# Attention values and scores of two pairs per visit in a fused attention and feed-forward kernel

## The chip, the core and the metric

The kernel runs on one core of a Trainium2 chip. The metric is the device time of one execution in microseconds (us). Engines are named as the profile names them: PE (TensorE, matmuls; PEld is its loading of weights), DVE (VectorE), ACT (ScalarE), POOL (GpSimd) and SP (SyncE, which issues most of the DMAs).

## What is computed

```python
def _attn_ref(q, k, v):                      # 8 x 8 heads x 576 x 64, float32
    scores = scale * np.matmul(q_c, k_c.transpose(0, 1, 2, 4, 3))   # in chunks of 64
    scores = scores - np.max(scores, axis=-1, keepdims=True)
    attn = np.exp(scores)
    attn = attn / (np.sum(attn, axis=-1, keepdims=True) + 1e-09)
    return np.matmul(attn, v_c)
def _moe_ref(x, w_in, w_out):                # 4608 x 512, 512 x 2048, 2048 x 512
    h = x @ w_in
    g = h - np.tanh(h)
    return g @ w_out
```

The attention is local: each chunk of 64 positions attends to itself alone. Its result, with the heads side by side, is the input x of the feed-forward part.

## The kernel before

The 4608 tokens are 36 **pairs** (two chunks of 64 tokens, 128 rows, with all 8 heads) and 9 **groups** of four pairs (512 tokens). Attention of a group runs one group ahead of its feed-forward part. Each float32 operand is split into a high and a low float16 part, and each matrix product is made of three of the four part products.

Up to the middle of group 2 all engines follow two orders written out by hand, as tokens (`PLAN` and `SECOND`). In `SECOND` the token `S16` is the scores of pair 16, `a17` the load of q and k of pair 17, `K13` a chunk, `gq3` the last product X5 of a unit, and so on. From group 3 (`LATER`) to group 8 the loops at L953 to L978 run, and there only PE's order is the order of the program text (`manual_schedule(engines={E.PE})`, L952). The other engines' orders are put together by the framework before the kernel runs, from what is ready and from the order of the text; each engine then works through its own queue strictly in that order.

A group has four **units** (`unit`, L750). The first feed-forward product uses seven products per quarter of the hidden columns instead of eight (Strassen and Winograd). They are named here by bank and first operand: Y1, X0, Z3, Z6, X4, Y2, X5 (`product`, L681, 12 matmuls of 256 columns each). X, Y and Z are three PSUM banks. X4 and X5 add to the sum in X, Z6 adds to Z; X0, Y1, Z3 and Y2 start anew. Four **shrinks** per unit (`shrink`, L690) take the sums out: `copied` (L705, ACT, from Y or Z), `summed` (L709, DVE, from X), `tanh` (L713, ACT), `less` (L717, DVE), `high` (L723, ACT) and `low` (L727, DVE). So X4 has to wait until shrink 0 has read X, X5 until shrink 1 has, and Z6 until `middle` (L679, ACT) has copied Z. A **chunk** (L731, 12 matmuls of 512 columns, two output tiles) is the second feed-forward product of one shrink's result, taken from a list that holds the results of three shrinks.

Between the third chunk and X5 stands the **attention visit** of pair p (L963 to L972):

- the values of p (`crossed_products`, L418): 48 matmuls of 64 x 64 (L427), into columns 256 to 511 of a pair of banks, of which one is Z and the other is used by attention alone;
- the scores of pair p + 1 (`scores`, L359; L183): 32 float32 matmuls in the trace, into columns 0 to 255 of the same two banks;
- the results of p (`results`, L442): a copy out of PSUM (L450, ACT), and sums and differences for x of the next group, split into parts (L454, L460 to L465, ACT and DVE);
- the softmax of p + 1: maxima (L374) and differences (L378) on DVE, exponentials (L387) on ACT, sums, reciprocals and products (L393 to L396) on DVE, high and low part (L405 on ACT, L410 on DVE), a transposing DMA (L415, SP);
- the loads of q and k of pair p + 3 (L304, SP).

At the start of the unit the values of p are split (L349 on ACT, L353 on DVE), and those of p + 4 are loaded (L308, SP); at its end their largest value is taken (L315, DVE), and once per group a power of two is made of these (`powers`, with an all-reduce on POOL, L116). Two buffers hold the split values, two the transposed shares, two the loaded q and k.

Of the kernel before, what the change touches and what calls it, by code (L numbers as in the profile page):

```python
# [52 lines left out]
"""  # L53

SECOND = """
v8 0i12 v9 W0.2 wA v11 0j12 x 0k12 0P14 xA 0G11 v10 0i11 0q12 wB 0P12 0j11 xB C0.0 W1.4 W1.8 W1.7 0k11 Cx1 C1.0 Cx0 0q11 f D0.0 Dx1 0P11 C1.6 Dx0 C0.1 G0 C0.3 D0.1 G1 D1.0 C1.3 e1 C1.5 C1.1 i0 D0.3 j0 C0.2 e0 D1.1 k0 C0.9 a8 C0.6 e2 G3 o1 u11 e3 q0 o0 W0.13 W0.10 P0 u10 u9 a9 i3 D0.6 i1 W1.10 j3 j1 k1 C0.5 u8 D1.6 q1 G6 C1.8 C1.7 W0.7 W0.8 k3 i6 D0.5 D1.3 C1.10 P1 M D0.9 C0.10 S8 o2 D1.5 W1.2 a10 G9 C1.9 j6 k6 C0.7 rA2 q3 P3 D1.10 i9 m8 D1.7 q6 E8 G5 C1.4 C0.13 j9 D0.2 P6 D0.7 k9 G7 C0.8 D1.9 W0.4 W1.13 W1.15 z8 rB2 T0.0.0 T0.0.1 D1.8 i5 q9 j5 W0.14 h8 C1.2 k5 T0.1.1 D0.10 D0.8 C0.4 l8 T0.1.0 C1.13 s8 t8 i7 W1.14 W0.15 s9 D1.2 S9 D1.13 T0.2.1 j7 m9 C0.14 q5 d8 fb P9 D0.13 G10 P5 k7 E9 z9 T0.3.1 T0.2.0 V8 G8 T0.3.0 i10 h9 j10 q7 D1.4 D0.4 P7 W0.12 s10 k10 q10 X8.0 i8 C1.14 C0.15 l9 c0.1 c0.2 d10 j8 D0.15 W1.12 W0.11 C0.12 C1.12 S10 G2 P10 t9 k8 i2 m10 b0.2 E10 q8 c0.0 D0.14 d9 G4 j2 k2 b0.1 V9 z10 P8 D1.12 X8.1 i4 a12 j4 q2 c0.3 h10 a11 X9.0 D1.14 G13 b0.0 s11 X9.1 C1.15 l10 S11 i13 X9.4 b0.3 v14 m11 T1.0.0 P2 X8.2 D0.12 o3 v13 T1.0.1 T1.2.1 X9.2 t10 X9.5 k4 q4 E11 W1.11 G15 i15 z11 X9.6 C1.11 d11 P4 j13 C0.11 v15 h11 l11 X9.7 k13 j15 V10 G14 i14 q13 k15 v12 P13 D1.15 t11 G12 X10.0 V11 u15 u12 T1.1.0 D0.11 j14 D1.11 k14 q15 X9.3 u13 X9.8 i12 X10.1 X11.0 T1.2.0 X10.2 T1.3.0 T1.1.1 q14 T1.3.1 P15 j12 k12 c1.3 u14 rA3 G11 S12 X11.1 q12 m12 X11.5 X11.2 P14 i11 a13 P12 E12 X11.3 rB3 c1.2 z12 j11 X11.4 gz0 s12 h12 k11 c1.0 X11.6 l12 gy0 q11 P11 t12 c1.1 sc0 mc0 ee2 b1.3 b1.0 b1.2 d12 b1.1 gx0 gu0 ee0 X11.7 ee3 V12 st0 sn0 X11.8 oo2 oo3 T2.0.1 su0 ee1 oo1 gv0 X12.0 sc1 a14 st1 gw0 sh0 T2.1.1 S13 sl0 gq0 sc2 T2.3.1 K0 m13 sn1 s14 st2 su1 sn2 sh1 gz1 su2 E13 sl1 z13 X12.1 h13 T2.2.1 st3 gy1 l13 sh2 T2.0.0 t13 sc4 d14 oo0 mc1 K1 s13 gx1 T2.2.0 sl2 sn3 T2.1.0 gu1 st4 T2.3.0 d13 sc5 K2 su3 X12.2 v18 sn4 c2.2 su4 V13 gv1 sh3 X13.0 sl3 sh4 c2.3 st5 gw1 sn5 sl4 K3 S14 c2.0 b2.2 c2.1 b2.3 v17 su5 X13.1 b2.0 gq1 m14 K4 sc6 v16 X13.2 E14 sh5 st6 b2.1 z14 st7 h14 sl5 l14 gz2 mc2 sn6 t14 gy2 a15 K5 u18 T3.0.0 su6 sn7 T3.1.0 T3.0.1 sh6 sc8 X13.4 T3.3.0 T3.1.1 sl6 T3.3.1 u16 gx2 T3.2.1 su7 st8 gu2 s15 u17 T3.2.0 sh7 K6 V14 gv2 sn8 su8 gw2 sc9 c3.0 sl7 sh8 d15 c3.2 sc10 X14.0 K7 st9 b3.0 c3.1 v19 sl8 S15 gq2 sn9 c3.3 K8 X14.1 b3.1 su9 m15 st10 b3.2 gz3 sh9 sl9 st11 sn10 E15 z15 h15 sn11 su10 l15 b3.3 u19 su11 a16 gy3 K9 sc12 mc3 sh10 t15 X13.3 X13.7 rA4 sl10 gx3 gu3 sh11 st12 X13.8 sc13 X13.5 sn12 K10 rB4 sl11 su12 X13.6 V15 gv3 X14.2 X15.0 X15.1 sh12 st13 X15.4 gw3 X15.5 X15.2 sn13 X15.7 X15.3 K11 S16 su13 gq3 sh13 sl12 X15.8 sl13 sc14 m16 st14 X15.6 st15 E16 K12 z16 sn14 sn15 su14 h16 sh14 su15 sh15 K13 a18 l16 sl14 sl15 t16 a17
"""

ORDER = (0, 1, 3, 6, 9, 5, 7, 10, 8, 2, 4, 13, 15, 14, 12, 11)
# [5 lines left out]
def attn_ffn_kernel(ctx: ExitStack, tc: tile.TileContext, qkE, vE, qL, kL, vL, w_in, w_out, out):  # L65
# [597 lines left out]
    class Winograd:  # L663
# [67 lines left out]
        def chunk(self, behind=3):  # L731
# [15 lines left out]
            if last:  # L747
                ff.finish(tiles)
# [277 lines left out]
```

## Time and profile before

| | |
|---|---|
| median of 3 runs | 793.89 us (793.58 to 794.11) |
| profiled execution, its own time | 793.73 us |
| its span, from the first to the last instruction | 792.0 us |
| PE busy | 784.5 us, 99% of the span |
| DVE busy | 610.8 us, 77% |
| ACT busy | 485.3 us, 61% |
| POOL busy | 47.9 us, 6% |

Busy time is the time in which at least one instruction of the engine ran. PE's matmuls overlap, and their ends are modelled, so PE's pace is read from the distance between starts and not from durations. A row of the timeline gives start and duration in us, engine, line, operation, output and inputs by the program's names, shapes and the number of instructions merged into it.

### The profile page before, as it was taken

How to read it: one execution, taken by the hardware profiler on the slowest of the kernel's cores; microseconds unless marked ns; L12 is line 12 of the kernel's file. 1: busy time of each engine (PE TensorE's matmuls, PEld its weight loads, DVE VectorE, ACT ScalarE, POOL GpSimd, SP SyncE). 2: the span in 40 equal slices, each digit the busy share in tenths (PEclk: the TensorE clock that was granted, in tenths of full speed). 3: DMA queues.
4: the chain of work that ended last, by engine and by line, in shares of the span. 5: the costliest groups of instructions: out<-in, count | busy, mean ns of one | idle time of the engine just before them, and what ended most of it. 6: DMA issues, size and time to landing. Idle time of an engine off the chain costs nothing.

```text
span 792.0 us, 17323 instructions
## 1 busy us (share of the span) xinstructions
PE 784.5 (99%) x7178; PEld 519.5 (66%) x7178; DVE 610.8 (77%) x1114; ACT 485.3 (61%) x938; POOL 47.9 (6%) x82
## 2 busy tenths in 40 slices
PE   8999999999999999999999999999999999999998
PEld 4877884444676666666666666666666666666664
DVE  8999999999999997676867686768676777654443
ACT  6989968986675655555645465556455645453443
POOL 0032135500000000000000000000000000000000
PEclk9999999999999999999999999999999999999999
DMA  9887848853131224111311131112211220001001
GB/s 355 321 234 220 222 130 179 150 134 81 28 111 50 81 61 108 47 55 54 108 55 54 55 105 37 50 40 92 68 55 41 68 67 15 15 12 43 1 1 54
DMA packets 58735, 72.43 MB, mean 91 GB/s; under 512 B 32800, under 2 KB 33056, under 8 KB 58528
## 3 DMA queue, kind: packets, MB, share of 16 engines
q1 hardware_dynamic: 53760, 61.81, 24.8%
q0 software_dynamic: 4752, 9.44, 7.0%
q8 instruction: 56, 0.92, 0.5%
q14 instruction: 23, 0.19, 0.1%
q10 hardware_dynamic: 144, 0.07, 0.0%
HBM read 45.09 MB, written 9.44 MB: 69 GB/s over the span
## 4 chain that ended last, share of the span: by engine, by line
PE 88%; DVE 7%; ACT 2%; DMA 2%; issue 1%; SPq 0%; DVEq 0%; ACTq 0%
PE po L746 36%; PE ph L687 23%; PE psa L687 9%; PE po L620 7%; PE ph L575 7%; PE psa L183 2%; PE psa L427 1%; DVE w L153 1%; DVE w L157 1%; DMA raw<-w_out 1%; PE psa L440 1%; DVE wl L164 1%; ACT junk L168 1%; DMA raw<-w_in 1%; DVE w L149 1%
## 5 line engine op out<-in xcount | busy, mean ns | idle before, releaser
L746 PE MATMUL po<-wl,gh 128*128 128x512 f16 x672 | 154.2, 379 | 0.0
L746 PE MATMUL po<-wl,gl 128*128 128x512 f16 (+1 forms) x672 | 151.6, 375 | 0.0
L687 PEld LDWEIGHTS <-wh 128*128 128x128 f16 x1344 | 129.2, 98 | 22.3
L687 PE MATMUL ph<-xh,wl 128*128 128x256 f16 x672 | 114.6, 273 | 0.0
L746 PEld LDWEIGHTS <-gl 128*128 128x128 f16 x720 | 69.1, 98 | 67.3
L687 PEld LDWEIGHTS <-wl 128*128 128x128 f16 x1008 | 98.5, 98 | 21.6
L746 PEld LDWEIGHTS <-gh 128*128 128x128 f16 x672 | 65.7, 98 | 67.3
L687 PE MATMUL ph<-xl,wl 128*128 128x256 f16 x336 | 91.6, 273 | 0.0
L687 PE MATMUL ph<-xh,wh 128*128 128x256 f16 x448 | 76.7, 273 | 0.0
L687 PE MATMUL psa<-xh,wh 128*128 128x256 f16 x448 | 76.4, 273 | 0.0
L620 PE MATMUL po<-wl,gh 128*128 128x512 f16 (+1 forms) x192 | 63.2, 383 | 0.0
L687 PE MATMUL ph<-xl,wh 128*128 128x256 f16 x224 | 61.1, 273 | 0.0
L687 PE MATMUL psa<-xl,wh 128*128 128x256 f16 x224 | 61.0, 273 | 0.0
L713 ACT ACTIVATE t<-t,sig 128x512 f32<-128x512 f32 x37 | 26.6, 719 | 32.9 <-DVE t L709 32.8
L713 ACT ACTIVATE t<-wh,sig 128x512 f32<-128x512 f32 x38 | 27.3, 720 | 31.0 <-DVE wh L709 30.9
L713 ACT ACTIVATE t<-spare,sig 128x512 f32<-128x512 f32 x37 | 26.6, 720 | 30.0 <-DVE spare L709 30.0
L575 PE MATMUL ph<-xl,wl 128*128 128x512 f16 x192 | 43.8, 379 | 0.2 <-DVE t L591 0.2
L454 ACT CAST xh<-wh 128x512 f16<-128x512 f32 (+1 forms) x56 | 31.4, 564 | 11.1 <-DVE wh L461 9.9
L709 DVE TENSOR_TENSOR wh<-ph,wh 128x512 f32<-128x512 f32 x28 | 19.3, 688 | 24.3 <-PE ph L687 24.1
L709 DVE TENSOR_TENSOR t<-ph,t 128x512 f32<-128x512 f32 x28 | 19.2, 687 | 23.4 <-PE ph L687 23.3
L387 ACT ACTIVATE s<-s 128x512 f32<-128x512 f32 x24 | 15.1, 629 | 36.0 <-DVE s L378 36.0
L717 DVE SCALAR_TENSOR_TENSOR wh<-wh,sig,t 128x512 f32<-128x512 f32 x38 | 28.4, 748 | 11.1 <-ACT t L713 11.0
(181 smaller groups left out, 1444.3 us busy)
## 6 DMA issues: line engine op xcount, KB each, us to landing
raw<-w_in SPq DMA_DIRECT2D x16, 512.0 KB, 6.0
raw<-w_out SPq DMA_DIRECT2D x16, 512.0 KB, 6.7
wh<-wl POOLq DMA_DIRECT2D x32, 256.0 KB, 4.2
rawv<-vL SPq DMA_DIRECT2D x28, 256.0 KB, 3.1
rawq<-qL SPq DMA_DIRECT2D x28, 256.0 KB, 3.1
rawk<-kL SPq DMA_DIRECT2D x28, 256.0 KB, 3.5
out<-wh SPq DMA_DIRECT2D x28, 256.0 KB, 2.1
qk<-qkE SPq DMA_DIRECT2D x8, 512.0 KB, 8.7
```

Source lines behind the costliest of these rows:

```text
L149: nc.vector.tensor_single_scalar(w, w, 3, op=ALU.logical_shift_left)
L153: nc.vector.scalar_tensor_tensor(out=w, in0=low, scalar=29, in1=w, op0=ALU.logical_shift_right, op1=ALU.bitwise_or)
L183: nc.tensor.matmul(ps[os, r ^ o if crossed else r, hp * CH:(hp + 1) * CH], lhsT=lhsT(rs, hp, o), rhs=rhs(rs, hp, o), start=True, stop=True)
L387: nc.scalar.activation(s, s, AF.Exp, scale=scale)
L454: return (lambda: nc.scalar.copy(out=h, in_=a)), (lambda: nc.vector.tensor_sub(l, a, h))
L575: nc.tensor.matmul(ph, lhsT=self.weight(fc, 0, a)[:, kc * P:(kc + 1) * P], rhs=x[b][:, kc, cols], start=(k == 0), stop=(k == 3 * KC - 1))
L620: nc.tensor.matmul(self.po[t], lhsT=gg[a][:, ts], rhs=self.weight(fc, 1, b), start=(k == 0), stop=(k == 3 * FC - 1))
L687: nc.tensor.matmul(bank[:, q * 2 * P:(q + 1) * 2 * P], lhsT=self.weight(u, a, i, q, kc), rhs=self.x[j][:, b, kc, :], start=(first and q == ...
L709: nc.vector.tensor_tensor(out=c, in0=self.banks["X"], in1=self.m5 if n % 4 == 3 else c, op=ALU.subtract if n % 4 == 2 else ALU.add)
L713: nc.scalar.activation(t, self.now[n][0], AF.Tanh, scale=self.ff.sig)
L717: nc.vector.scalar_tensor_tensor(out=c, in0=c, scalar=self.ff.sig, in1=t, op0=ALU.mult, op1=ALU.subtract)
L746: nc.tensor.matmul(bank, lhsT=g[a][:, ts], rhs=half_w[1][fc][:, b, columns], start=(first and s == 0 and k == 0), stop=(last and s == 1 an ...
```

## The change

The visit takes two pairs, p and p + 1, in every second unit, and stands at the end of the unit, behind the last chunk: first the values of both, then the scores of the next two. The values of a pair go into one half of the columns of X and one half of Y (pair p in the first, p + 1 in the second), and the copy out of PSUM becomes two of 256 columns. The scores of an odd pair go into columns 256 to 511 of the two banks of the scores. Maxima and differences stand ahead of all steps of the results but the copies out. Splits, loads and largest values come for two pairs at a time; `powers` comes in the third unit of a group instead of the fourth. In the unit the chunks move: one at the start, one cut into two halves (one output tile each) around Z3, one behind Z6, and one at the end; X4 comes ahead of Z6. In `SECOND`, pair 17 gets its load and scores (`a17`, `S17`), and its softmax follows the hand-written part.

```diff
-... u19 su11 a16 gy3 ... K11 S16 su13 gq3 ... sl14 sl15 t16 a17
+... u19 su11 a16 a17 gy3 ... K11 S16 S17 su13 gq3 ... sl14 sl15 t16
...
-        def scores(self, p):
+        def scores(self, p, second=False):
...
-            d["ps"] = quarters(self.two_banks(), lambda r, hp, c: q[r, hp, c, :], lambda r, hp, c: k[r, hp, c, :], "u", self.crossed(p))
+            ps = self.two_banks()
+            d["ps"] = quarters(ps[:, :, 4 * CH:] if second else ps, lambda r, hp, c: q[r, hp, c, :], lambda r, hp, c: k[r, hp, c, :], "u", self.crossed(p))
...
-        def crossed_products(self, p):
+        def crossed_products(self, p, banks):
...
-                        nc.tensor.matmul(ps[os, c, hp * CH:(hp + 1) * CH], lhsT=v[a][rs, c, hp, :], rhs=d["a16"][rs, b, hp, cs], start=(k == 0), stop=(k == 2), skip_group_check=True)
+                        nc.tensor.matmul(banks[c][os, hp, :], lhsT=v[a][rs, c, hp, :], rhs=d["a16"][rs, b, hp, cs], start=(k == 0), stop=(k == 2), skip_group_check=True)
...
+                halves = to.rearrange("p s k (c t) -> p (s k) c t", c=2)
+                return [lambda c=c: nc.scalar.mul(halves[:, :, c], bank[c], 2.0 ** -14) for c in range(2)]
...
-        def chunk(self, behind=3):
+        def chunk(self, behind=3, parts=(0, 1)):
...
             extra("start")
+            self.chunk()
             self.product("Y", u, 1, 1, True)
-            self.chunk()
             self.product("X", u, 0, 0, True)
             self.shrink(u, 0)
+            self.chunk(parts=(0,))
             self.product("Z", u, 3, 3, True)
             self.middle()
+            self.chunk(parts=(1,))
+            self.product("X", u, 4, 4)
+            self.product("Z", u, 6, 2)
+            self.shrink(u, 1)
             self.chunk()
-            self.product("Z", u, 6, 2)
-            self.product("X", u, 4, 4)
-            self.shrink(u, 1)
             self.product("Y", u, 2, 6, True)
-            self.chunk()
-            extra("attention")
             self.product("X", u, 5, 5)
             self.shrink(u, 2)
             self.shrink(u, 3)
             self.chunk()
+            extra("attention")
             extra("end")
...
+    att.softmax(CROSSED + 1)
+    att.transpose(CROSSED + 1)
+    att.load(CROSSED + 3)
...
+                    if u % 2 or p >= NPAIR:
+                        return
+                    two = p, p + 1
+                    later = [n for n in (p + 2, p + 3) if n < NPAIR]
+                    if where == "start":
+                        for n in two:
+                            att.split(n)
+                            att.load_values(n + 4)
+                    elif where == "attention":
+                        for n in two:
+                            att.crossed_products(n, [w.banks[b].rearrange("p (n hp k) -> n p hp k", n=2, hp=4)[n % 2] for b in "XY"])
+                        for n in later:
+                            att.scores(n, n % 2 == 1)
+                        rest = []
+                        for n in two:
+                            steps_ = att.results(n, nx)
+                            for f in steps_[:2]:
+                                f()
+                            rest += steps_[2:]
+                        for n in later:
+                            att.less(n)
+                        for n in later:
+                            att.load(n + 2)
+                        for f in rest:
+                            f()
+                        for n in later:
+                            att.exponents(n)
+                            att.shares(n)
+                            att.transpose(n)
+                    elif where == "end":
+                        for n in two:
+                            att.largest(n + 4)
+                        if u == 2 and later:
+                            att.powers(g + 2)
```

## Rows read from the trace of the kernel before

**Rows 1.** The page, parts 1 and 2: busy time, granted clock of PE.

```profile
PE 784.5 (99%) x7178; PEld 519.5 (66%) x7178; DVE 610.8 (77%) x1114; ACT 485.3 (61%) x938; POOL 47.9 (6%) x82
...
PEclk9999999999999999999999999999999999999999
```

**Rows 2.** The chain that ended last, from 440 to 470 us, by line.

```profile
by line: PE po L746 51.8%; PE ph L687 30.9%; PE psa L687 14.2%; PE psa L183 1.9%; PE psa L427 1.7%
```

**Rows 3.** Timeline of PE from a unit's third chunk on: start, duration, engine, line.

```profile
446.58 2.75 PE L746 MATMUL po<-wl,gl 128*128 128x512 f16 x12
449.27 0.58 PE L427 MATMUL psa<-wh,wh 64*64 64x64 f16 x48
449.72 0.69 PE L183 MATMUL psa<-rawk,rawq 64*64 64x64 f32 x32
450.35 0.39 PE L687 MATMUL ph<-xh,wh 128*128 128x256 f16 x2
...
451.67 2.75 PE L746 MATMUL po<-wl,gh 128*128 128x512 f16 x12
454.26 0.38 PE L687 MATMUL ph<-xh,wl 128*128 128x256 f16 x2
...
455.57 2.75 PE L746 MATMUL po<-wl,gl 128*128 128x512 f16 x12
```

**Rows 4.** Line 450 after 297 us, one per pair: shortest, median, longest ns.

```profile
L450 ACT ACTIVATE wh<-psa x20: 577/578/600, 305.4 to 698.5; 128x512 f32<-128x512 f32 x20
```

**Rows 5.** Timeline of PE, stretches ending at 449.36, 449.65, 449.86 and 450.15 us.

```profile
449.27 0.28 PE L427 MATMUL psa<-wh,wh 64*64 64x64 f16 x11
...
449.27 0.57 PE L427 MATMUL psa<-wh,wh 64*64 64x64 f16 x47
...
449.72 0.35 PE L183 MATMUL psa<-rawk,rawq 64*64 64x64 f32 x9
...
449.72 0.65 PE L183 MATMUL psa<-rawk,rawq 64*64 64x64 f32 x29
```

**Rows 6.** Timeline of DVE behind the same visit.

```profile
451.30 0.42 DVE L460 TENSOR_TENSOR wh<-wh,wh 128x256 f32<-128x256 f32 x1
451.64 0.42 DVE L464 TENSOR_TENSOR wh<-wh 128x256 f32<-128x256 f32 x1
...
456.58 0.67 DVE L393 TENSOR_REDUCE sm<-s 128x8 f32<-128x512 f32 x1
457.17 0.74 DVE L717 SCALAR_TENSOR_TENSOR spare<-spare,sig,t 128x512 f32<-128x512 f32 x1
457.83 0.16 DVE L394 TENSOR_SCALAR sm<-sm 128x8 f32<-128x8 f32 x1
457.95 0.75 DVE L717 SCALAR_TENSOR_TENSOR t<-t,sig 128x512 f32<-128x512 f32 x1
458.62 0.20 DVE L395 RECIPROCAL sm<-sm 128x8 f32<-128x8 f32 x1
```

**Rows 7.** Timeline of ACT behind the same visit.

```profile
449.88 0.72 ACT L349 ACTIVATE wh<-rawv,to 128x512 f16<-128x512 f32 x1 [1.34 <-PE psa L427]
450.51 0.58 ACT L450 ACTIVATE wh<-psa 128x512 f32<-128x512 f32 x1
451.12 0.41 ACT L454 CAST xh<-wh 128x256 f16<-128x256 f32 x1
...
456.10 0.72 ACT L713 ACTIVATE t<-spare,sig 128x512 f32<-128x512 f32 x1
```

**Rows 8.** Timeline of DVE where the hand-written part ends.

```profile
293.62 0.75 DVE L727 SCALAR_TENSOR_TENSOR gl<-wh,to_g,gl 128x512 f16<-128x512 f32 x1
```

**Rows 9.** Timeline of PE there: Z3 of the first unit of group 3.

```profile
293.64 0.38 PE L687 MATMUL psa<-xh,wh 128*128 128x256 f16 x2
```

**Rows 10.** DMA issues after 297 us: median us from issue to landing.

```profile
wh<-wh SPq DMA_TRANSPOSE x19, 3.1
```

**Rows 11.** Groups of POOL after 297 us: busy us, mean ns, idle before.

```profile
L116 POOL PARTITION_ALL_REDUCE xtop<-tops x4 | 1.5, 371 | 312.3 <-DVE tops L323 312.3
```

More of the change, by code (lines that the diff above doesn't have):

```diff
@@ L456, in results @@
             if p % 2 == 0:
-                return [out(first), *parts(0, first)]
+                return [*out(first), *parts(0, first)]
             def between():
@@ L465, in others @@
                 nc.vector.tensor_sub(t34[:, 1], t12[:, 1], first[:, 1])
-            return [out(second), between, *parts(3, t12), others, *parts(2, second[:, 1:2]), *parts(5, t34)]
+            return [*out(second), between, *parts(3, t12), others, *parts(2, second[:, 1:2]), *parts(5, t34)]
     class Half:
@@ L740, in chunk @@
             for c, t in enumerate(tiles):
+                if c not in parts:
+                    continue
                 for bank, columns in ff.columns(t):
@@ L746, in chunk @@
                             nc.tensor.matmul(bank, lhsT=g[a][:, ts], rhs=half_w[1][fc][:, b, columns], start=(first and s == 0 and k == 0), stop=(last and s == 1 and k == 2))
-            if last:
+            if last and 1 in parts:
                 ff.finish(tiles)
@@ L959, in extra @@
                 def extra(where):
-                    if where == "start" and p < NPAIR:
-                        att.split(p)
-                        att.load_values(p + 4)
-                    elif where == "attention" and p < NPAIR:
-                        att.products(p)
-                        if p + 1 < NPAIR:
-                            att.scores(p + 1)
-                        for f in att.results(p, nx):
-                            f()
-                        if p + 1 < NPAIR:
-                            att.softmax(p + 1)
-                            att.transpose(p + 1)
-                            att.load(p + 3)
-                    elif where == "end" and p < NPAIR:
-                        att.largest(p + 4)
-                        if u == UNITS - 1 and p + 1 < NPAIR:
+                    if u % 2 or p >= NPAIR:
[22 more added lines that the diff above has]
+                        for f in rest:
+                            f()
+                        for n in later:
[6 more added lines that the diff above has]
+                        if u == 2 and later:
                             att.powers(g + 2)
```

21 lines of the change are left out of this document (10 added, 11 removed).

## The prediction

> **What bounds the kernel now.** I read the page's first two parts, then the chain that ended last over the repeating part, then TensorE's timeline of one unit. The first parts say that TensorE (PE) is busy for 99% of the span at the full clock [rows 1]; VectorE, at 77%, is next. Busy time alone proves little, since overlapping matmuls count as busy, so the chain matters more: from 440 to 470 us it consists of PE alone [rows 2]. The timeline then gives PE's real rate, as distances between starts. A chunk takes 451.67 to 454.26 = 2.59 us, a product 454.26 to 455.57 = 1.31 us [rows 3]. A unit has 4 chunks and 7 products, 10.36 + 9.17 = 19.53 us, at the same rate wherever I looked, with no wait of PE on another engine. What is left of a unit is the attention visit. In it the chunk before lasts 446.58 to 449.27 = 2.69 us, 0.10 more than usual; 48 small matmuls of the values take 0.45; 32 of the scores take 0.63; the product after takes 1.32, 0.01 more [rows 3]. So a visit costs 0.10 + 0.45 + 0.63 + 0.01 = 1.19 us of PE, and there are 20 of them [rows 4], 19 with scores (the last pair has no successor). Only two things can move the end: a shorter visit, or a new wait of PE.
>
> **The merged visits.** No matmul is added or removed; 20 visits become 10. How much of 1.19 us is paid per visit and how much per matmul? Inside the values, 11 matmuls had started by 449.36 and 47 by 449.65 [rows 5]: 36 in 0.29 us, 8.1 ns each, so that 48 in the middle of a burst cost 0.39 us. Inside the scores, 9 had started by 449.86 and 29 by 450.15 [rows 5]: 14.5 ns each, so 32 cost 0.46 us. The second pair of a visit thus adds 0.39 + 0.46 = 0.85 us instead of 1.19, and each merging saves 0.10 + 0.06 + 0.17 + 0.01 = 0.34 us. The ten merged value bursts save 10 x 0.17 (entry, values, exit); the scores save 0.17 ten times too, nine times in the visits and once where S17 now follows S16. Sum: -3.4 us.
>
> The bounds of this term: if every small matmul cost its average share (0.45/48, 0.63/32) in any company, only entry and exit would go, 10 x 0.11 = -1.1 us. I take the slope inside the bursts, because there I see the cost of the next matmul directly. The TensorE page of the Trainium skill ("TensorE: Matmul & The Clock Gate", Part 1, "Wait — 56ns, not 53.3ns?") says that starts are never closer than about 25 ns, however small the matmul. By that rule a pair would cost 80 x 25 = 2.0 us (an estimate from that page) and nothing inside a burst could be saved; the trace does not agree, with 8.1 and 14.5 ns.
>
> **Values in X and Y.** The value matmuls now overwrite the banks of two running products, so they wait for the last reads of them. I count from the next start after the product X5 (t = 0). Its sums for shrinks 2 and 3 are two VectorE slots of 0.60 [rows 6], done at about 1.6; the values start at 2.59 + 0.10 = 2.69, behind the chunk. Cost nothing; the cover is that chunk, with 1.1 us to spare. Values then end at 2.69 + 0.45 + 0.39 = 3.53, scores at 3.53 + 0.63 + 0.46 = 4.62. ScalarE copies the results out in halves of 256 columns, two per pair, of 0.41 each (by L454 of that width) instead of one copy of 0.58 [rows 7], 0.24 us more per pair. It first has tanh and high of shrinks 2 and 3, 4 x 0.72 from about 0.9, so it is free at 3.8 and done at 5.4. The next Y product starts behind its own chunk, at 4.62 + 2.59 = 7.21, and X at 8.52. Cost nothing, 1.8 us to spare.
>
> **Scores of both pairs in Z and the fourth bank.** The Z product needs the two maxima and differences done. They start at 4.8 (scores' end and a little) and take 4 x 0.60, to 7.2. Z is due at 8.52 + 1.31 + 1.30 (half a chunk) = 11.13. Even if they came behind all sums of the results (3.5 us, below) they would be done at 10.7. Cost nothing, so the request to put them first is worth little here.
>
> **The new order of chunks and products.** The matmuls are the same; what changes is the cover of each chain. X5 must wait for shrink 1's sum: copy and addition, 0.58 and 0.75 at most, against a chunk and a product, 3.9 us. The first chunk of a unit uses shrink 1 of the unit before: six steps of 0.6 to 0.75, about 4.5 us, against chunk, Y, X5, chunk, 7.8 us. The tight one is X4, which overwrites X: it waits for shrink 0's sum and has half a chunk, Z3 and half a chunk, 1.30 + 1.31 + 1.30 = 3.91 us, where it had Z3, a chunk and Z6 (5.2 us), and now in the shadow of two pairs' attention work on VectorE. X0 ends at 9.83, X4 is due at 13.73. VectorE's work for the visit, from 4.8 on: maxima and differences 4 x 0.60 = 2.40; results 0.60 + 4 x 0.34 + 0.60 + 0.34 + 0.60 = 3.50; sum, add, reciprocal, product and low part of two softmaxes 2 x (0.60 + 0.12 + 0.12 + 0.60 + 0.60) = 4.08 [rows 6]. In all 9.98, so 14.8. Shrink 0's sum has to start by 13.05. It does if at least 1.75 us of that work stands behind it. The two low parts (1.20) wait for ScalarE's casts at the end anyway; and today VectorE never runs two dependent softmax steps back to back: sum, L717, add, L717, reciprocal [rows 6], a shrink step in each hole. So I take no stall; the price otherwise is a rival below.
>
> **S17, loads, transposes, POOL.** S17 moves ahead of X5 of the hand-written part: its 0.46 us of PE is in the sum above, and its loads go ahead on SP behind those of pair 16, into buffers that S15 has left. The new wait at the seam: maxima and differences of pair 17 come at the end of the hand-written VectorE order, which ended at 293.62 + 0.75 = 294.37 [rows 8], so at 295.6; Z was at 293.64 [rows 9], and gets 0.46 for S17 and 1.30 for half a chunk on top: 295.4. I put 0.2 us, once (0 to 1.2). Per visit SP issues four loads, two value loads and two transposes at once instead of half of that twice; a transpose lands in 3.1 us [rows 10], and its reader is the visit 41 us later. Queued behind them on SP are only output stores. POOL's four all-reduces of 0.37 us [rows 11] come a unit earlier, with a whole unit of cover instead of the gap between two units. The results of a group's last pairs also come a unit sooner. All this costs nothing; the waits that PE has before a visit are more in number, and I bound their issue at 0 to 0.5 us in all.
>
> **Sum.** -3.4 + 0.2 + 0.2 = -3.0 us. The profiled execution took 793.73 us (span 792.0), 0.16 under the median of 793.89; so 790.7 on its own scale, **790.9** against the median.
>
> **Rivals.**
>
> A. VectorE's backlog stalls X4 (the other side). Place: behind each of the nine visits with scores. Price: if all of the 9.98 us goes first, the sum runs from 14.8 to 15.5, X4 starts 1.75 us late, 9 x 1.75 = 15.8 us, 806.7. If only the two low parts stay behind it, it ends at 14.3, 0.55 us late, 5.0 us, 795.9. It decides from 13.05 on. For it: two pairs can fill each other's holes, which one pair cannot, and attention stands before the next unit in the program text. Against it: the interleaving in [rows 6], and that the second pair's steps need ScalarE too. Chance: 0.17 for the severe form (over 0.6 us per visit), 0.17 for the mild one, between 791.5 and 796.
>
> B. The fixed part does not go, cost follows the count of small matmuls: -1.1 + 0.4, so 793.2. Against it: the slopes of [rows 5]. Chance 0.07. The 25 ns of the Trainium skill's page speak for this rival, and [rows 5] against that page.
>
> C. Y waits for the results. Today ScalarE runs the next value split (L349, 0.72) ahead of the result copy (L450) [rows 7]. If two of these go first, 5.4 becomes 6.8, still before 7.21; with one step more, 7.6, 0.4 us late, ten times: +4.0, 794.9. Chance 0.05. "Perfetto Trace Analysis" of the Trainium skill (Optimizing Tensor Performance, Matmuls) asks for independent groups to rotate through different banks, so that one is emptied beside the next. This change gives that up for X and Y.
>
> D. The change is not in effect. PE's order is written by hand, so the merging is certain; only the request on VectorE may be ignored, and that was worth nothing above. Under 0.01.
>
> **How the numbers follow.** 0.2% (about 1.6 us) is what a measurement of this kernel can tell from no change. Forecast without stalls, 790.1 to 792.2: 0.54, faster. Mild A: 0.03 faster, 0.12 same, 0.02 slower. B and C, 0.12: same, 0.10, and 0.02 slower. Severe A: 0.17 slower. In all 0.57 faster, 0.22 same, 0.21 slower. The range 790.0 to 796.0 leaves out severe A and little else.
>
> **What would show it.** Right: visits every 41 us, values (96) in about 0.84 us, scores (64) in about 1.1, no other distance between starts changed. Wrong: a start of X4 (second X product) later than 1.30 us after the second half chunk began, with VectorE's L709 as the one waited for (A); 0.9 and 1.26 us in the bursts (B); a late Y behind L450 (C).

## The result and the profile after

| | before | after |
|---|---|---|
| median | 794.07 us (793.58 to 794.78) | 799.5 us (798.45 to 800.97) |
| ratio of the times | | 1.0071, 95% interval 1.0058 to 1.0084 |
| profiled execution | 793.73 us, span 792.0 | 798.45 us, span 796.7 |

The change made the kernel slower; the forecast was 790.9 us, and the time lies above the range. Each kernel's sum below is made against the span of its own profiled execution, so the change cost 796.7 - 792.0 = 4.7 us there. (The profiled execution was the shortest of six; the medians differ by 5.4 us, and what the other executions lost beyond 4.7 no trace shows.) In one execution of the experiments, the profiled one of "splits behind the softmax and copy of Z ahead of the tanh together", the matmuls of the chunks took 673 to 677 ns in the mean instead of 375 to 379 and the whole 1643.6 us; the ratios leave it out.

First the page of after: engines, granted clock, chain of waits by engine.

```profile
PE 782.8 (98%) x7174; PEld 519.1 (65%) x7178; DVE 612.4 (77%) x1114; ACT 484.7 (61%) x958; POOL 48.9 (6%) x82
...
PEclk9999999999999999999999999999999999999999
...
PE 75%; DVE 17%; ACT 4%; issue 2%; DMA 2%; POOL 0%; SPq 0%; POOLq 0%; DVEq 0%; ACTq 0%
```

Work and clock are those of [rows 1]; but the chain now passes through DVE and ACT. Before, it was:

```profile
PE 88%; DVE 7%; ACT 2%; DMA 2%; issue 1%; SPq 0%; DVEq 0%; ACTq 0%
```

The groups of PE's instructions from 290 to 792 us name the waits (last column: idle time of PE and what ended it; it leaves out a part of each wait, since a matmul's modelled end hides it):

```profile
L750 PE MATMUL po<-wl,gh 128*128 128x512 f16 x588 | 139.0, 379 | 0.2 <-DVE gh L727 0.2
L750 PE MATMUL po<-wl,gl 128*128 128x512 f16 (+1 forms) x591 | 133.8, 375 | 1.0 <-issue 1.0
...
L687 PE MATMUL psa<-xh,wh 128*128 128x256 f16 x384 | 65.5, 273 | 1.0 <-ACT m L679 1.0
L687 PE MATMUL ph<-xh,wh 128*128 128x256 f16 x384 | 65.5, 272 | 1.6 <-DVE spare L709 0.8 <-DVE t L709 0.6
...
L183 PE MATMUL psa<-rawk,rawq 64*64 64x64 f32 x576 | 10.8, 221 | 1.2 <-issue 1.2
```

In the kernel before, the same groups sat idle for 0.0 us. Measured between starts (a wait is what a distance exceeds the usual 0.216 us of a chunk's matmul or 0.109 of a product's, or the 1.09 us of 64 scores), the waits of after are:

| late | ended by | where | us |
|---|---|---|---|
| X4 | shrink 0's sum, L709 | behind 6 of 9 visits, 0.37 to 0.51 | 2.4 |
| X5 | shrink 1's sum, L709, which stands behind a wait for POOL (L123) | 3 times 0.25 | 0.75 |
| Z6 | copy of Z, L679 | 0.66 and 0.62 | 1.3 |
| half chunk at the seam | low part, L727 | once | 0.4 |
| scores, or the chunk behind them | nothing the profile shows | 3rd, 6th, 9th visit: 1.53, 0.93, 0.40 | 2.9 |
| sum | | | 7.7 |

The gain is there too. The timeline of PE at the second visit of after:

```profile
348.66 1.89 PE L750 MATMUL po<-wl,gh 128*128 128x512 f16 x8
350.48 0.25 PE L427 MATMUL ph<-wh,v16h 64*64 64x64 f16 x8
...
350.88 0.63 PE L427 MATMUL ph<-wh,wh 64*64 64x64 f16 x48
351.38 1.16 PE L183 MATMUL psa<-rawk,rawq 64*64 64x64 f32 x64
352.47 1.47 PE L750 MATMUL po<-wl,gl 128*128 128x512 f16 x6
```

Eight matmuls of 0.216 from 348.66 end at 350.39, so the entry costs 0.09, the 96 values 351.38 - 350.48 = 0.90, the 64 scores 1.09, the exit 0.01 as before: 2.09 us for what took 2 x 1.19. That is 0.29 per merging, about -2.9 in ten. And -2.9 + 7.7 = 4.8, against 4.7 measured.

**Why X4 is late.** VectorE and ScalarE of after, behind the first visit (scores end at 310.70, X4 due at 319.82):

```profile
310.65 0.74 DVE L353 SCALAR_TENSOR_TENSOR v16l<-rawv,to,v16h 128x512 f16<-128x512 f32 x1
311.31 0.74 DVE L353 SCALAR_TENSOR_TENSOR wh<-rawv,to,wh 128x512 f16<-128x512 f32 x1
312.29 0.42 DVE L460 TENSOR_TENSOR wh<-wh,wh 128x256 f32<-128x256 f32 x1 [0.23 <-ACT wh L450]
...
315.70 0.69 DVE L379 TENSOR_TENSOR s<-psa,mx 128x512 f32<-128x512 f32 x1
...
318.19 1.27 DVE L394 TENSOR_REDUCE sm<-s 128x8 f32<-128x512 f32 x2
319.38 0.16 DVE L395 TENSOR_SCALAR sm<-sm 128x8 f32<-128x8 f32 x1
319.45 0.69 DVE L709 TENSOR_TENSOR t<-ph,t 128x512 f32<-128x512 f32 x1
```

```profile
309.85 0.71 ACT L349 ACTIVATE v16h<-rawv,to 128x512 f16<-128x512 f32 x1
310.47 0.70 ACT L349 ACTIVATE wh<-rawv,to 128x512 f16<-128x512 f32 x1
311.08 1.18 ACT L450 ACTIVATE wh<-ph 128x256 f32<-128x256 f32 x4
...
320.18 0.73 ACT L713 ACTIVATE t<-t,sig 128x512 f32<-128x512 f32 x1 [2.13 <-DVE t L709]
320.81 0.56 ACT L679 COPY m<-psa 128x512 f32<-128x512 f32 x1
```

```profile
320.19 0.38 PE L687 MATMUL ph<-xh,wh 128*128 128x256 f16 x2 [0.21 <-DVE t L709]
```

The two value splits for the next visit (L353, and L349 on ScalarE) stand first in both queues: they become possible when this visit's value matmuls have read the buffers. Up to L460 they and the wait behind them take 312.29 - 310.65 = 1.64 us. Then come results and maxima, then L709 at 319.45, 0.37 us too late for X4. And ScalarE's copy of Z stands behind the tanh of shrink 0, which waited 2.13 us for that same L709: so Z6 depends on VectorE too.

**Why X5 is late.** VectorE behind the same visit, a product later (X5 due at 326.71, started at 326.96):

```profile
325.96 0.16 DVE L123 TENSOR_REDUCE from<-xtop 128x1 f32<-128x4 f32 x1 [0.57 <-POOL xtop L116]
326.15 0.15 DVE L125 TENSOR_SCALAR from<-from 128x1 f32<-128x1 f32 x1
326.22 0.68 DVE L709 TENSOR_TENSOR wh<-ph,wh 128x512 f32<-128x512 f32 x1
```

Shrink 1's sum stands in the queue behind L123 of `powers`, which waits 0.57 us for POOL's all-reduce. This happens four times, and X5 is late behind three of them.

**The waits of the third visit.** The scores stop two matmuls before their end, take 395.57 - 392.95 = 2.62 us instead of 1.09, and no engine releases them (after, timeline of PE):

```profile
392.95 1.15 PE L183 MATMUL psa<-rawk,rawq 64*64 64x64 f32 x62
395.32 0.33 PE L183 MATMUL psa<-rawk,rawq 64*64 64x64 f32 x2 [1.22 <-issue]
```

The DMA view of 392 to 394 us shows one packet alone:

```profile
q8 instruction: 1, 0.02, 3.1%
```

It is an instruction load: 56 such packets of 16 KB stand against 7178 + 7174 instructions of PE, 256 each. This one starts at 392.92 and takes 0.98. PE goes on 2.40 us after its start, and in the other two cases 2.36 and 2.35 us. The stops lie at instructions 7052, 9606 and 12160 in order of start, ten blocks apart but for six. A merged visit has 320 PE instructions in 2.0 us, more than a block, where a single one had 160 in 1.1.

### The profile page after: what moved, and what is told of

The parts are those of the page before. It is cut to its first block, busy times and chain, and to the rows that moved or that the text cites. A ratio compares the mean times of both kernels' runs of the same rounds, so it can differ in the third digit from the quotient of the medians.

```text
span 796.7 us, 17340 instructions
## 1 busy us (share of the span) xinstructions
PE 782.8 (98%) x7174; PEld 519.1 (65%) x7178; DVE 612.4 (77%) x1114; ACT 484.7 (61%) x958; POOL 48.9 (6%) x82
## 4 chain that ended last, share of the span: by engine, by line
PE 75%; DVE 17%; ACT 4%; issue 2%; DMA 2%; POOL 0%; SPq 0%; POOLq 0%; DVEq 0%; ACTq 0%
PE po L750 29%; PE ph L687 19%; PE psa L687 8%; PE ph L575 8%; PE po L620 7%; DVE xl L454 2%; DVE mx L375 1%; PE ph L427 1%; DVE s L379 1%; ACT wh L450 1%; PE psa L183 1%; DVE w L153 1%; DVE w L157 1%; DVE tops L315 1%; PE psa L438 1%
## 5 line engine op out<-in xcount | busy, mean ns | idle before, releaser
L750 PE MATMUL po<-wl,gh 128*128 128x512 f16 x672 | 158.3, 379 | 0.2 <-DVE gh L727 0.2
L687 PEld LDWEIGHTS <-wh 128*128 128x128 f16 x1344 | 130.8, 98 | 30.8 <-issue 5.1
L709 DVE TENSOR_TENSOR wh<-ph,wh 128x512 f32<-128x512 f32 x28 | 19.3, 689 | 34.5 <-PE ph L687 17.6
L709 DVE TENSOR_TENSOR spare<-ph,spare 128x512 f32<-128x512 f32 x28 | 19.3, 689 | 32.7 <-ACT spare L705 16.7
L709 DVE TENSOR_TENSOR t<-ph,t 128x512 f32<-128x512 f32 x28 | 19.3, 689 | 31.5 <-PE ph L687 16.2
L717 DVE SCALAR_TENSOR_TENSOR t<-t,sig 128x512 f32<-128x512 f32 x37 | 27.6, 745 | 10.3 <-ACT t L713 10.0
```

Of the source, the lines that this page charges most:

```text
L687: nc.tensor.matmul(bank[:, q * 2 * P:(q + 1) * 2 * P], lhsT=self.weight(u, a, i, q, kc), rhs=self.x[j][:, b, kc, :], start=(first and q == ...
L709: nc.vector.tensor_tensor(out=c, in0=self.banks["X"], in1=self.m5 if n % 4 == 3 else c, op=ALU.subtract if n % 4 == 2 else ALU.add)
L717: nc.vector.scalar_tensor_tensor(out=c, in0=c, scalar=self.ff.sig, in1=t, op0=ALU.mult, op1=ALU.subtract)
L750: nc.tensor.matmul(bank, lhsT=g[a][:, ts], rhs=half_w[1][fc][:, b, columns], start=(first and s == 0 and k == 0), stop=(last and s == 1 an ...
```

## The experiments

Each is the changed kernel with the edit shown, unless said otherwise. "Late" is between starts, as above.

**Splits behind the softmax.** `last_act` and `last_dve` are the previous visit's last cast and low part of the shares (L406, L411).

```diff
-                            att.split(n)
+                        with tc.issue_after(att.last_act.ins), tc.issue_after(att.last_dve.ins):
+                            for n in two:
+                                att.split(n)
```

> The changed kernel, but the value splits for the next visit (L349 on ACT, L353 on DVE) are queued behind the visit's softmax. Theory 1, VectorE's and ScalarE's queue behind a visit is too long for X4, and the two splits (1.33 us of VectorE, 1.24 of ScalarE) are the part that was not counted: the late X4 (0.37 us in six of nine visits), the late Z6 (0.6 us, twice) and the late X5 (0.25 us, three times) go, 4.4 us in all, and the stalls in the middle of a burst or a chunk stay: about 795.1 against 799.5 for the changed kernel. Theory 3, the new order of products in the unit leaves X4 too little cover whatever the queue holds: X4 stays late by about 0.4 us, 799.

797.47 us (795.23 to 798.25, where 795.1 was expected), ratio 1.0038 (1.0025 to 1.0052); span of the profiled execution 793.5. Late X4, X5 and Z6 are gone from the second visit on. In the first unit Z6 is 0.23 late; the first visit has its values 0.57 late, perhaps since its first split was put back too, then X4 0.49 and Z6 0.43. The stops without a releaser remain, 1.83 and 0.91. So the late X4, X5 and Z6 behind the visits come from the splits' place in the queues.

**Half a chunk between values and scores**, to cut the burst; `chunk` and its second half stay in order, the other half following behind the scores.

```diff
+                        if later:
+                            w.chunk(parts=(0,))
+                            w.cut = True
```

> The changed kernel, but half of the next unit's first chunk stands between the values and the scores of a visit. Theory 2, PE runs out of loaded instructions because a visit uses up more than one 256-instruction block (16 KB) in 2 us: the three stalls of 1.37, 0.93 and 0.40 us inside bursts and chunks go (2.7 us), a second entry into the scores costs 0.10 to 0.17 us nine times; 798 against 799.5. If those stalls are waits on another engine's result instead, they stay or move to the same instruction: 800.5. The late X4 stays or grows a little, since the maxima come 1.3 us later.

806.38 us, 1.0161 (1.0147 to 1.0175). The stops shrink from 2.9 to 1.1. But the scores end 1.3 us later, and nobody had reckoned with the Z products:

```profile
L687 PE MATMUL psa<-xh,wh 128*128 128x256 f16 x384 | 65.4, 272 | 9.6 <-DVE s L379 6.0 <-ACT m L679 3.6
```

Z3 waits 0.93 us for the differences behind six visits (0.33 to 1.20 behind the others), Z6 0.56 for the copy behind all nine.

**Both of these** edits together.

> The splits behind the softmax and half a chunk between values and scores, both. Theories 1 and 2 together: all 7.1 us of stalls but the one at the seam go, 1.2 us of entries come: 799.5 - 7.1 + 1.2 = 793.6, no worse than the kernel before (794.1). If either theory is wrong, above 796.

799.76 us, 1.0076 (1.0064 to 1.0089). Z3 still waits 0.62 to 0.65 for L379 behind six visits, 1.72 behind the first; the stops are 0.74 and 0.88. Freeing VectorE gives back 6.6 us, but not the cover of Z3.

**Results first:** the requested order of maxima and results undone.

```diff
+                        for f in rest:
+                            f()
                         for n in later:
                             att.less(n)
...
-                        for f in rest:
-                            f()
```

> The changed kernel with one part undone: the results' sums and differences are asked for ahead of the maxima and differences of the next scores, as in the kernel before. The prediction's account (behind all sums of the results the differences would be done at 10.7 us, the first Z product due at 11.1): no late Z3, no change beyond 1 us against the changed kernel. Rival 1 (VectorE's backlog holds more than was counted, the splits among it): Z3 waits for the differences of the second pair, 0.5 to 1.5 us in each of nine visits, 804 to 812. Rival 2 (shrink 0's sum profits when Z3 is late): X4 is on time instead, and the sum is near zero again.

806.33 us, 1.0152 (1.0137 to 1.0168): rival 1. The group of Z3 in it, and its queue:

```profile
L687 PE MATMUL psa<-xh,wh 128*128 128x256 f16 x384 | 65.5, 272 | 10.4 <-DVE s L379 10.4
```

```profile
311.70 0.75 DVE L353 SCALAR_TENSOR_TENSOR wh<-rawv,to,wh 128x512 f16<-128x512 f32 x1
...
317.96 0.67 DVE L315 TENSOR_REDUCE tops<-rawv 128x1 f32<-128x512 f32 x1
318.56 0.68 DVE L379 TENSOR_TENSOR s<-psa,mx 128x512 f32<-128x512 f32 x1
```

The second differences end at 319.2, Z3 was due at 317.6: 1.68 late at five visits, 0.59 to 1.49 at three. Ahead of them stand the splits and one of the largest values (L315, 0.6). X4 is never late in this kernel, and its stops are 1.83 and 1.08. The request that I called worth little is worth about 0.8% between the two ratios.

**One pair per visit** in every unit, in the new order of the unit, with the values in X and Y, and without `S17` ahead: the new order without the merging.

```diff
-                    two = p, p + 1
-                    later = [n for n in (p + 2, p + 3) if n < NPAIR]
+                    later = [n for n in (p + 1,) if n < NPAIR]
```

> One pair per visit in every unit as before, without S17, but in the changed kernel's unit order, with the visit at the unit's end, values in X and Y and the maxima ahead of the results' sums. Theories 1 and 2, the cost comes from two pairs at once: no late X4 and no stall in a burst, 794.1 like the kernel before, within 1 us. Theory 3, the unit order is at fault: X4 late by about 0.4 us behind each of 19 visits, 801.

801.5 us, 1.0094 (1.008 to 1.0108). No stops without a releaser, no late X4, but Z6 is 0.28 to 0.51 late behind 17 visits and 0.86 behind one, for the copy of Z:

```profile
L687 PE MATMUL psa<-xh,wh 128*128 128x256 f16 x384 | 65.4, 272 | 4.2 <-ACT m L679 4.0
```

**The same with the copy of Z ahead of shrink 0's tanh** on ScalarE.

```diff
-            self.shrink(u, 0)
+            self.copied(4 * u)
+            self.summed(4 * u)
...
-            self.middle()
+            with tc.issue_after(self.middle().ins):
+                for f in (self.tanh, self.less, self.high, self.low):
+                    f(4 * u)
```

> The single-pair run, but on ScalarE the copy of Z stands ahead of shrink 0's tanh. If Z6 was late because that copy stood in line behind a tanh that waits for VectorE's sum, its 0.3 to 0.5 us (19 times, 7 us) go: about 794.5 against 801.5. If the copy itself takes too long in the new unit order, whatever stands ahead of it: 801 again.

794.78 us, 1.0008 (0.9999 to 1.0017). Not one Z6 is late; one X4 of 0.46 in the first unit is left, where the chunk around Z3 falls out and Z3 alone covers it. So with X4 ahead of Z6, the new order put an in-order queue with a waiting tanh in front of Z6, and that alone costs 6.7 us when every unit has a visit.

**Values and scores in turn:** values of two pairs at the end of even units, scores of the next two at the end of odd ones.

```diff
-                    if u % 2 or p >= NPAIR:
+                    if p >= NPAIR:
...
+                    even = u % 2 == 0
+                    two = (p, p + 1) if even else (p - 1, p)
+                    later = [n + 2 for n in two if n + 2 < NPAIR]
```

> The changed kernel with the values of two pairs at the end of the even units and the scores of the next two at the end of the odd units. No burst holds more than 192 PE instructions, and each unit has about half of the backlog on VectorE. Merging alone, with one more entry per two units: 10 x 1.01 + 9 x 1.25 + 0.46 = 21.8 us of small matmuls against 23.0 before, 792.8 if no wait of PE is left. By theory 2 no stall in the middle of a chunk or burst. By theory 3 as the single-pair run showed it (Z6 waits for the copy of Z, which stands on ScalarE behind a tanh that waits for VectorE) a late Z6 of about 0.3 us in up to 19 units: 798.

793.21 us, 0.9988 (0.9979 to 0.9997), a little faster than the kernel before. Only the 0.40 at the seam is left, and the chain is PE's again:

```profile
PE 88%; DVE 8%; ACT 2%; DMA 1%; issue 1%; SPq 0%; DVEq 0%; ACTq 0%
```

**Scores ahead of the last chunk, values behind it**, splits behind the softmax.

```diff
+            extra("scores")
             self.chunk()
             extra("attention")
```

> The changed kernel with the scores and their maxima and differences ahead of the unit's last chunk, the values behind it, and the value splits queued behind the softmax (from the second visit on). A chunk of 2.6 us lies between the two bursts: by theory 2 no stall from instruction loading. VectorE's backlog starts 2.7 us earlier: by theory 1 no late X4 and no late Z6. 792.8 as in the spread run. If the maxima push shrink 2's and 3's sums back, the values wait for X instead: 0.6 us nine times, 798.

812.77 us, 1.0233 (1.0219 to 1.0247). Here the wait of rival C shows, 2.06 us behind each of the nine visits with scores: Y1 waits for the copies of the results.

```profile
L687 PE MATMUL ph<-xh,wl 128*128 128x256 f16 x576 | 96.9, 272 | 17.1 <-ACT wh L450 17.1
```

X5 is late twice as well, 0.60 and 0.69. There is no stop without a releaser.

**A shift of the blocks:** 64 small idle matmuls more at the start, 128 PE instructions.

```diff
+    for _ in range(64):
+        nc.tensor.matmul(idle[:, :8], lhsT=warm[:, :P], rhs=warm[:, :8], start=True, stop=True)
```

> The changed kernel with 64 small matmuls (128 PE instructions) more at the very start, nothing else. In the changed kernel the stalls inside a burst or chunk sit at the third, sixth and ninth visit, each time at the same instruction count modulo 256. By theory 2 the shift of 128 moves them to the second, fifth and eighth visit (about 1.4 us each) and leaves a small one (up to 0.4) at the first; none at the third, sixth and ninth. If they are waits for data of those visits, they stay where they were.

801.63 us in one execution (span 799.8). The stops moved: none at the third, sixth and ninth visit, 1.41 at the fifth, 0.86 at the eighth, none at the second, where I had expected one. The late products stayed.

**Splits behind the softmax and copy of Z ahead of the tanh together** (from the second visit on for the splits).

```diff
+                            if p > CROSSED:
+                                behind.enter_context(tc.issue_after(att.last_act.ins))
+                                behind.enter_context(tc.issue_after(att.last_dve.ins))
...
+            with tc.issue_after(self.middle().ins):
+                for f in (self.tanh, self.less, self.high, self.low):
+                    f(4 * u)
```

> The changed kernel with two alterations of the order of the queues alone: the value splits queue behind the softmax of the visit (from the second visit on), and ScalarE's copy of Z stands ahead of the tanh of shrink 0. Theory (late X4, X5 and Z6 come from what stands ahead of them in the queues of VectorE and ScalarE): no late X4, X5 or Z6 from the second visit on, and the first one at most 0.5 us; left are the seam (0.4) and the instruction-loading stalls, about 2.5 us; with -2.7 of merging the time is 794 to 795.5. Rival 1 (the new order of the unit is too short of cover whatever the queues do): X4 or Z6 late by 0.3 us or more per visit still, 797 or more. Rival 2 (the loading stalls are waits for operands in disguise): they go too, and the time is 792 or less.

795.07 us, 1.0011 (1.0002 to 1.002). It was run once more for its trace:

> The kernel with the value splits behind the softmax and the copy of Z ahead of the tanh once more, for its trace. It took 1.0 us more than the kernel before (795.07 against 794.1). Theory: the starts of PE show no late X4, X5 or Z6 from the second visit on, the seam 0.4, one late product in the first unit, and 2 to 3 us of instruction-loading stalls in the visits or the chunk behind them, a whole number of 256-instruction loads apart. Rival: Z6 or X4 late by 0.2 to 0.4 us per visit, and loading stalls under 1 us.

Span 792.6. There are no stops without a releaser, against my expectation. Late are X4 of the first unit (1.39) and, behind every second visit, X4 by about 0.1 and Z6 by 0.43; 4.1 us in all. The result of shrink 0 now enters the list later: in the first unit the chunk around Z3 falls out here too, so that X4 has 1.31 us of cover instead of 3.9. That chunk comes behind the first visit instead of ahead of it, and every visit begins 24 PE instructions earlier against the blocks.

**The last chunk cut in two around the values**, on top of that.

```diff
-            self.chunk()
+            self.chunk(parts=(0,))
+            extra("values")
+            self.chunk(parts=(1,))
             extra("attention")
```

> As the kernel with splits and copy of Z reordered, and besides the unit's last chunk is cut in two: first half, values of both pairs, second half, scores of the next two. No work is added, and the scores end where they did. Theory (loading stalls come where more than 256 PE instructions go in less time than one load takes): the burst of 320 is cut into 192 and 128 with 1.3 us between, and the stalls fall from about 2.5 us to under 0.6; against that, entering a burst costs 0.1 us a second time in each visit (1.0), and the values, 1.3 us earlier, may wait up to 0.3 us per visit for the sum of shrink 3 out of X. Time within 1.5 us of the other one, 793 to 796. Rival (they go with the number of instructions, whatever the density): still 2 us or more of stalls in the visits or the chunk behind them, 796 to 798.

804.91 us, 1.0135 (1.0121 to 1.0148); neither account gave that time. It has one stop, 0.65, where the kernel without the cut has none, so this says nothing for cutting the burst. The values wait 0.23 per visit for shrink 3's sum (0.32 with the usual entry), as expected, but with the results earlier in the queues X5 is late by 0.73 to 1.56 at three visits and Z6 by 0.43 to 0.88 at eight.

**The shares asked for behind the copy of Z**, on top of splits and copy of Z; in the first unit shrink 0 is as in the changed kernel. `pending` holds the pairs whose exponentials are under way.

```diff
                             att.exponents(n)
-                            att.shares(n)
-                            att.transpose(n)
+                        pending.extend(later)
...
+                    if where == "middle":
+                        while pending:
+                            n = pending.pop(0)
+                            att.shares(n)
+                            att.transpose(n)
```

> The kernel with the splits behind the softmax, in which besides the sums, reciprocals, products and parts of the new shares are asked for behind the next unit's copy of Z, so that ScalarE's cast of a share no longer stands ahead of that copy. In the first unit the order of shrink 0 is the changed kernel's, so that its visits begin at the same instruction numbers as there. Theory of queues: no late X4, X5 or Z6 behind any visit; left is the seam (0.4 to 0.6). Theory of instruction loading (what counts is where a visit lies against the blocks of 256 instructions): stalls of 2 to 3 us in all come back at the third, sixth and ninth visit, as in the changed kernel, and the time is 793.5 to 795. Rival (the loading stalls went with the queues' waits, not with the place): none, and 791 to 792.5.

794.01 us, 1.0003 (0.9994 to 1.0011), no stops. X4 is 1.21 late behind the first visit, where the chunk around Z3 falls out and Z3 alone covers it. Z6 is still late by 0.29 to 0.38 at every second visit: the request changed the text, and the framework still put the cast ahead of the copy.

**The same with a chunk of the first unit left to the end.**

```diff
             self.shrink(u, 1)
-            self.chunk()
+            self.chunk(99 if seam else 3)
```

> The same with one chunk of the first unit (the one behind Z6) left to the end of the program, so that every visit begins 24 PE instructions earlier against the blocks; nothing else. Theory of instruction loading: no stalls, as in the kernel of which only the trace was looked at again, and the time is 1.5 to 3 us below the other kernel's of this pair, 791 to 792.5; X5 of the first unit may be late by up to 0.5. That is the forecast's sum without stalls, -2.7 and a seam. Rival: stalls as in the other kernel, and the same time within 0.5 us.

794.24 us, 1.0005 (0.9996 to 1.0014). From the second visit on both kernels stand alike against the blocks, since the first one lost a chunk ahead of its second visit by itself. The pair tells nothing apart.

**The changed kernel with that chunk left out alone**, the other edits undone.

> The changed kernel with one chunk of the first unit of group 3 (the one behind Z6) left to the end of the program, so that each visit begins 24 PE instructions earlier against the blocks of 256; nothing else is altered. Theory of instruction loading (what counts is where a visit lies against the blocks): the 1.37, 0.93 and 0.40 us at the third, sixth and ninth visit go, the late X4, X5 and Z6 stay as they are, X5 of the first unit may be late by 0.3: 796.5 to 797.5 where the changed kernel has 799.5 in the median (its profiled run 798.45, so 796 here). Rival (they belong to the visits' waits, which are as before): stalls of 2 us or more in all stay, and the time is within 0.7 us of the changed kernel's.

801.83 us, 1.01 (1.0086 to 1.0113). The stops are gone (no group of PE has idle time ended by issue), as the account by place said. The time is not as expected: the framework makes new queues for the other engines when PE's order changes, and in these L709 comes later.

```profile
L687 PE MATMUL psa<-xh,wh 128*128 128x256 f16 x384 | 65.5, 273 | 1.3 <-ACT m L679 1.0 <-DVE s L379 0.3
L687 PE MATMUL ph<-xh,wh 128*128 128x256 f16 x384 | 65.4, 272 | 5.8 <-DVE t L709 2.1 <-DVE wh L709 1.9 <-DVE spare L709 1.3
```

X4 is late by 0.39 to 1.15 at each of nine visits: rival A near its severe form, from 24 instructions' difference.

**The shares bound behind shrink 0's sum and the copy of Z**, on top of the shares asked for there.

```diff
+                        with ExitStack() as behind:
+                            behind.enter_context(tc.issue_after(w.last_sum.ins))
+                            behind.enter_context(tc.issue_after(w.last_copy.ins))
                             while pending:
```

> The kernel that asked for the shares behind the copy of Z, with that order now binding on the queues: sums, reciprocals, products and parts of the new shares stand behind shrink 0's sum on VectorE and behind the copy of Z on ScalarE. Theory of queues: Z6 is no longer late by 0.38 us behind every second visit, nor X4 by 1.21 in the first unit; left are the seam (0.42) and at most 0.3 elsewhere, so the span is 792.0 - 2.7 + 0.7 = 790.0 and the time 791.5 to 792.5, below the kernel before by 0.2 to 0.3%. Rival (cover is short elsewhere too): a new late product behind each visit, 793.5 or more.

792.96 us, 0.9988 (0.9979 to 0.9997): the best time, level with that of values and scores in turn, and some 0.5 us above what the theory gave. ScalarE at the third visit:

```profile
399.99 0.59 ACT L679 COPY m<-psa 128x512 f32<-128x512 f32 x1 [0.58 <-PE psa L687]
402.51 1.22 ACT L406 CAST wh<-s 128x512 f16<-128x512 f32 x2 [1.94 <-DVE s L397]
403.64 0.72 ACT L713 ACTIVATE t<-wh,sig 128x512 f32<-128x512 f32 x1
```

The copy goes before cast and tanh, and no Z6 is late. Left are X4 behind the first visit (1.13, again with Z3 as its only cover), the seam (0.41), and X5 by 0.10 to 0.18.

**The sum over the traces.** The time from the first product of the feed-forward part (209.5 to 210.1 us in these traces) to PE's last matmul, against the kernel before, less the waits counted by starts, is what the merging brought: 5.0 - 7.7 = -2.7 (after), 8.0 - 10.7 = -2.7 (chunk left), 0.8 - 4.1 = -3.3 (splits and copy of Z), -0.1 - 3.1 = -3.2 (shares behind), -1.0 - 2.3 = -3.3 (shares bound). In the first two, most values of a visit take 0.90 us, in the last three 0.85.

## Why the prediction was wrong

The forecast was -3.4 us of merging and 0.4 of new waits. The merging came, nearly in full; the new waits were 7.7 us: instruction loading 2.9, X4 2.4, Z6 1.3, X5 0.75, the seam 0.4. The prediction had none of these but the seam in its sum.

**The merged visits: right, and a little short in the changed kernel.** I took 0.34 per merging, -3.4 in all; the visit shows 0.29, -2.9. The scores came as forecast (1.09 for 1.1), the values not: 0.90 instead of 0.84, the figure given for rival B. But this is not the higher cost of each matmul that rival B meant. Three distances near the end of the 96 values, 18, 34 and 25 ns where 8 or 9 is usual, make up the 0.05 us. In the kernel with the splits behind the softmax, and in the last three of the sum above, they are gone from most visits, the values take 0.85 us, and a merging saves the 0.34 of the forecast. What causes the three distances is not shown. The rule of about 25 ns per start ("TensorE: Matmul & The Clock Gate", Part 1, "Wait — 56ns, not 53.3ns?" of the Trainium skill) does not hold here either: 96 values in 0.90 us are 9.4 ns each.

**The failed step: the queue in front of shrink 0's sum** ("The new order of chunks and products"). I counted 9.98 us for VectorE and asked for 1.75 of it to stand behind the sum. That much did: reciprocals, one addition, products and low parts, 2.7 us, come behind L709 in the trace. But the list held the visit's work only. The splits for the next visit had been in view in [rows 7], ahead of the result copy, and I used them in rival C, on ScalarE alone; their VectorE half, and the wait for the copies they hold up, are 1.64 us in front of everything. L709 starts 319.45 - 308.70 = 10.75 us after the first value, and X4 needs it by 10.38 (319.1 us, the 13.05 of the prediction). With the splits behind, it starts at 9.73 at the second visit (361.17 - 351.44), some 0.6 in time. The largest values (L315, L323), which now come in pairs, were not in the list either. The experiment with the splits behind removes the late X4 from the second visit on, so this is shown. What came is rival A, in its mild form, at six visits of nine.

**Z6 was left out.** The prediction has no line on its new wait. With X4 ahead of it, it comes one product after Z3's cover, and its copy stands on ScalarE behind a tanh that waits for VectorE. The pair of single-visit kernels shows it as 6.7 us; in the changed kernel it cost 1.3, perhaps because X4's own wait gave the copy time.

**X5 and the all-reduce.** The prediction gave X5 3.9 us of cover for copy and addition, and put POOL's all-reduces, a unit earlier, at nothing. What it left out is again the queue: `powers` now stands in front of shrink 1's sum with a wait of 0.57 us, and X5 was late three times by 0.25. With the splits behind the softmax that sum comes first (326.12, L123 at 331.85), and X5 is on time. In the kernel before, the trace shows the same wait 2.4 us ahead of the next L709, at no cost.

**Scores in Z: the time right, the reason wrong.** Z3 was never late in the changed kernel. But "the request to put them first is worth little" was wrong by some 6 us: the 0.4 us that I reckoned left for Z3 without it (11.13 - 10.7) did not exist, for the same splits and a largest value.

**Values in X and Y: right.** They never waited in the changed kernel, nor did Y1 for the results (rival C). Both covers are real ones: values half a chunk earlier wait 0.23 at each visit, and where the scores and their maxima went ahead of the values, the copies of the results came 2.06 too late for Y1.

**The seam** cost 0.4 where I put 0.2, within 0 to 1.2, but at a half chunk waiting for the last low part [rows 8], not at Z3.

**A term that was missing: instruction loading,** 2.9 us of 7.7. Nothing in the kernel before shows it, and no bound of mine covered it. Without it the profiled execution would have ended near 795.6, inside the range; the median, less the same 2.9, at 796.6, still outside.

## What to carry to other kernels

When a visit is merged, write out the whole queue of each engine from the visit to the tightest product, with the work that the visit *releases* (here the splits for the next one), and look for instructions that wait while others stand behind them; a request in the program text does not bind a framework that plans the queues, an explicit "behind this instruction" does. Halving the number of bursts doubles what each queue must pass at once: ask of each cover whether it held for one portion or for two. A small gain on the bounding engine, 0.29 us per visit here, is undone by one late product of the same size in each.

## What the hardware showed that was not expected

A burst of small matmuls can outrun instruction loading. The three stops end 2.35 to 2.40 us after the load starts, whose packet takes about 1 us. The 256 PE instructions ahead of them took 1.64, 2.16 and 3.20 us; a unit's chunks and products take 19.5 us for 264. All stops, in the seven traces that have any, lie at the same place in a block: 129 to 145 in order of start, modulo 256. The shift by 128 instructions moved them to other visits, and leaving 24 instructions out ahead of the visits removed all of them in an otherwise unaltered program text. In the kernel before, with 160 instructions per burst, PE's groups show no idle time at all. The Trainium skill ("Runtime: NRT & Kernel Launch", "Instruction fetch mechanics") says that streams are refilled in 16 KiB blocks of 256 instructions and that crossing a boundary is mostly hidden, because instructions are issued slower than they are loaded. The size agrees with the 56 packets here; the hiding holds in chunks and products, and not in or just behind these bursts, where it cost 1.53, 0.93 and 0.40 us. What spares a visit is not settled: after the shift by 128 instructions there was none at the second visit, where I had expected one.
